# A decode kernel's weight stream: row 31 of wo on another queue, and fifteen marking loads

## The chip, the cores and the metric

The kernel runs on one core of a Trainium2 chip. The metric is the device time of one execution in microseconds (us). The kernel before takes 101.78 us, the median of two runs (101.76 and 101.81). One more execution was recorded by the hardware profiler; its span, from the first to the last instruction, is 100.0 us (100.03).

## What is computed

One token (batch 1, sequence 1, width 1024) goes through a layer with two parallel branches. Cut to what matters:

```python
xn = layernorm(x)
# branch A: attention over the last W = 4096 cached positions, 32 query heads, 4 key/value heads
q = xn @ wq
p = softmax(q . k / sqrt(128));  o = p . v
a = o.reshape(1, 1, 4096) @ wo
# branch B: an MLP, 1024 -> 3584 -> 1024
h = gelu(layernorm(xn) @ w1 + b1)
b = h @ w2 + b2
out = x + a + b
```

All tensors are bf16. With one token every weight is used once, so the kernel reads some 40 MB from memory and does little with each byte.

## The kernel before

**The stream.** SP issues all large loads in one order: the keys (L72), wq in two halves (L81), w1 in two halves (L207), the values (L213), w2 in two halves (L221), wo in two halves (L229). Each large tile is one of four buffers of a ring, so a load waits until an earlier user of its buffer is done; the second half of wo, for instance, takes the buffer that L320 (`o_all`) has read. ScalarE issues three small loads (x, b2, b1) at the start.

**wo and the end.** wo is seen as 128 partitions x 32 rows of 1024, and a row of it (256 KB, 2 KB in each partition) is one step of the final product: `o8[:, c]` against row c. The first half, rows 0 to 15, is one load of 4 MB. The second half, rows 16 to 31, comes in five pieces, cut at 8, 12, 14, 15 and 16, so that the last pieces are small. The list `chunk_src` names the rows in the order in which TensorE uses them: 28 rows of w2, then rows 0 to 31 of wo. All but the last four are summed in `accf` (L341), each row as two products of 512 columns. That sum is copied out (L345 on ScalarE, L346 on VectorE) while the last four rows (`TAIL = 4`, L357) go into fresh sums `acct`, each row as four products; four more products at L353 bring one part of the copied sum back in, before the row next to the last. L361 and L362 make the result, and two halves of the output, 1 KB each, are written by SP (L364) and ScalarE (L365). The program ends (L391) when each queue has seen its landings and the engines have met.

**GpSimd.** It makes small constants at the start and takes part in the two layer norms: `rstd` (L145) and `rstd2` (L168). Between these two stand three selects (L110, L115, L117). VectorE's `yT` (L170) waits for `rstd2`, and behind it on VectorE stand the transposes of the keys (L186) and the copies into `kT` (L202).

**Who sets the order.** Each engine and each queue runs its instructions in order. The tile framework places the instructions of a queue and adds a wait on a semaphore wherever an instruction touches bytes that an earlier one writes; a load's semaphore is raised when its data have landed.

Of the kernel before, what the change touches and what calls it, by code (L numbers as in the profile page):

```python
# [9 lines left out]
BF16 = mybir.dt.bfloat16  # L10
# [6 lines left out]
def kernel(  # L17
# [14 lines left out]
    nc = tc.nc  # L32
    P = 128
    D = A_x.shape[-1]
# [13 lines left out]
    CWO = NQ // P  # L48
# [5 lines left out]
    consts = ctx.enter_context(tc.tile_pool(name="consts", bufs=1))  # L54
# [8 lines left out]
    def ring_tile(name):  # L63
        return ring.tile([P, RING_ELEMS], BF16, tag="ring", name=name, align_bytes=256)
# [13 lines left out]
    for i in range(2):  # L78
        t = ring_tile(f"wq{i}")
        tv = t[:].rearrange("p (r n) -> p r n", r=4)  # L80
# [88 lines left out]
    yT = consts.tile([P, C], BF16)  # L169
    nc.vector.tensor_scalar(out=yT[:], in0=xn_f[:], scalar1=mean2[:], scalar2=rstd2[:], op0=ALU.subtract, op1=ALU.mult)  # L170

    accf = ps_acc.tile([P, 512], FP32, tag="accf")
    nc.vector.memset(accf[:], 0.0)
    accq = ps_acc.tile([P, 2, 512], FP32, tag="accq", name="accq")
# [15 lines left out]
    for g in range(Hkv):  # L190
        T4 = scr[:, g, :].rearrange("p (c a j) -> p c a j", a=4, j=32)
        k = 0
# [11 lines left out]
    for i in range(2):  # L204
        t = ring_tile(f"w1{i}")
        tv = t[:, :4 * Fd].rearrange("p (r n) -> p r n", r=4)
# [8 lines left out]
    chunk_src = []  # L215
    w2_v = B_w2.rearrange("(p c) n -> p c n", p=P)
    for i in range(2):
        nr = CW2 // 2
        t = ring_tile(f"w2{i}")
        tv = t[:, :nr * D].rearrange("p (r n) -> p r n", r=nr)  # L220
        nc.sync.dma_start(out=tv, in_=w2_v[:, nr * i:nr * (i + 1), :])  # L221
        chunk_src += [("h", nr * i + r, tv[:, r, :]) for r in range(nr)]
    wo_v = A_wo.rearrange("(p c) n -> p c n", p=P)
    for i, cuts in enumerate([[0, 16], [0, 8, 12, 14, 15, 16]]):
        nr = CWO // 2
        t = ring_tile(f"wo{i}")
        tv = t[:].rearrange("p (r n) -> p r n", r=nr)
        for a, b in zip(cuts[:-1], cuts[1:]):
            nc.sync.dma_start(out=tv[:, a:b, :], in_=wo_v[:, nr * i + a:nr * i + b, :])  # L229
        chunk_src += [("o", nr * i + r, tv[:, r, :]) for r in range(nr)]  # L230


    for i, w3 in enumerate(wq_tiles):
        for r in range(4):
            c = 4 * i + r
# [16 lines left out]
    for i, w3 in enumerate(w1_tiles):  # L252
        for r in range(4):
            c = 4 * i + r
# [141 lines left out]
```

## Time and profile before

| what | value |
|---|---|
| median of the runs | 101.78 us |
| profiled execution, its span | 100.0 us |
| bytes read from memory | 39.86 MB |
| SP's queue, share of 16 DMA engines over the span | 93.6% |
| busy share: PE, VectorE, ScalarE, GpSimd | 51%, 50%, 34%, 4% |
| last wait of SP for its own output's landing | 0.6 us |

The page gives busy time by engine, the span in 40 slices, and the chain of waits that ended last. The DMA engines are busy in nearly every slice, the compute engines only in some. Times inside the span count from its start. A group row names the line, the engine, the operation, the tiles and the idle time before it with what ended it.

### The profile page before, as it was taken

To read this page: it belongs to the slowest core of one execution; us is meant where nothing else is said; L and a number is where in the kernel's file an instruction comes from. 1 tells how busy PE (TensorE), PEld (TensorE's weight loads), DVE (VectorE), ACT (ScalarE), POOL (GpSimd) and SP (SyncE) were. 2 spreads that over 40 slices of the span, in tenths; PEclk is the share of its full clock that TensorE was granted. 3 is DMA by queue.
4 is the path that set the end of the run, shared out by engine and by line. 5 is a ranking of instruction groups with operands and counts; after the bars stand their busy time and mean duration, and the time that the engine had idled before them with its cause. 6 is when DMAs were issued, how large, how long until landed. Compare 5 with 4: busy or idle time off the path is not lost.

```text
span 100.0 us, 970 instructions
## 1 busy us (share of the span) xinstructions
PE 51.2 (51%) x365; PEld 20.0 (20%) x365; DVE 49.7 (50%) x92; ACT 34.1 (34%) x37; POOL 3.8 (4%) x16
## 2 busy tenths in 40 slices
PE   0065200008500940193892935999469950199980
PEld 0042200002100310031530322334123410033320
DVE  5445499999999999997125115410450000000021
ACT  5000002999999999962001044400000000000010
POOL 6005200000000000000000000000000000000000
PEclk9999999999995579555555555559985998557999
DMA  2999999999999999998999999999999999999920
GB/s 26 394 420 426 491 488 472 419 419 419 432 419 393 401 500 382 413 482 378 390 429 426 429 531 390 413 477 390 459 447 426 419 432 419 406 419 411 401 73 1
DMA packets 2878, 39.92 MB, mean 399 GB/s; under 512 B 309, under 2 KB 311, under 8 KB 698
## 3 DMA queue, kind: packets, MB, share of 16 engines
q1 hardware_dynamic: 2866, 39.85, 93.6%
q8 instruction: 3, 0.05, 0.2%
q10 hardware_dynamic: 8, 0.01, 0.0%
q14 instruction: 1, 0.01, 0.0%
HBM read 39.86 MB, written 0.00 MB: 398 GB/s over the span
## 4 chain that ended last, share of the span: by engine, by line
DVE 38%; DMA 24%; PE 21%; issue 9%; POOL 3%; ACT 2%; SPq 1%; POOLq 1%; ACTq 0%
DMA wo<-in_A_wo_dram 24%; DVE kt_scr L186 17%; DVE kT L202 16%; PE o_all L320 10%; PE sp L276 4%; PE acch L258 3%; ACT e L298 1%; DVE eTb L300 1%; PE qT_ps L262 1%; DVE m_loc L284 1%; PE acct L357 1%; SPq L229 1%; DVE q_sb L241 1%; POOLq L391 1%; POOL spread L110 1%
## 5 line engine op out<-in xcount | busy, mean ns | idle before, releaser
L200 ACT COPY kT<-kt_scr 32x1024 bf16<-32x1024 bf16 x26 | 27.1, 1042 | 14.8 <-DVE kt_scr L186 14.5
L186 DVE STREAM_TRANSPOSE kt_scr<-k_sb 128x4096 bf16<-128x4096 bf16 x4 | 17.4, 4411 | 0.0
L238 PE MATMUL accq<-wq,xnT 128*1 128x512 bf16 x64 | 7.1, 622 | 18.3 <-DMA wq<-in_A_wq_dram 18.3
L202 DVE COPY kT<-kt_scr 32x1024 bf16<-32x1024 bf16 x38 | 15.9, 419 | 0.5
L346 DVE COPY bulk<-accf 33x320 f32<-33x320 f32 x1 | 0.5, 483 | 21.9 <-ACT bulk L345 21.9
L341 PE MATMUL accf<-wo,o 128*1 128x512 bf16 x56 | 8.3, 459 | 6.0 <-DMA wo<-in_A_wo_dram 5.9
L345 ACT COPY bulk<-accf 33x192 f32<-33x192 f32 x1 | 0.3, 312 | 31.9 <-PE accf L341 31.9
L320 PE MATMUL o_all<-v_sb,eTb 128*32 128x512 bf16 x32 | 10.0, 491 | 1.0 <-DVE zcol L311 1.0
L258 PE MATMUL acch<-w,yT 128*1 128x448 bf16 x64 | 6.3, 572 | 6.0 <-DMA w<-in_B_w_dram 6.0
L341 PE MATMUL accf<-w,hT 128*1 128x512 bf16 x56 | 7.9, 451 | 0.0
L238 PEld LDWEIGHTS <-xnT 128*1 128x1 bf16 x64 | 2.1, 116 | 22.5 <-issue 22.4
L320 PEld LDWEIGHTS <-eTb 128*32 128x32 bf16 x32 | 3.8, 120 | 6.9 <-issue 3.9
L341 PEld LDWEIGHTS <-o 128*1 128x1 bf16 x56 | 2.8, 97 | 11.4 <-issue 9.2
L258 PEld LDWEIGHTS <-yT 128*1 128x1 bf16 x64 | 2.0, 115 | 9.8 <-issue 9.8
L276 PE MATMUL sp<-kT,qm 128*32 128x512 bf16 x32 | 3.8, 630 | 0.3 <-DVE qm L267 0.3
L341 PEld LDWEIGHTS <-hT 128*1 128x1 bf16 x56 | 2.7, 96 | 4.7 <-issue 2.5
L323 DVE TENSOR_TENSOR o_m<-o_all,grs 32x512 f32<-32x512 f32 x1 | 0.7, 680 | 5.8 <-PE o_all L320 5.8
L123 PE MATMUL x_ps<-ones_bf,xb 1*128 1x1 bf16 x8 | 0.7, 200 | 5.0 <-DMA xb<-in_A_x_dram 5.0
L298 ACT ACTIVATE e<-sc,nmx 128x1024 bf16<-128x1024 f32 x1 | 1.1, 1148 | 5.7 <-DVE nmx L295 5.7
L315 DVE STREAM_TRANSPOSE hT<-h_sb 128x896 bf16<-128x896 bf16 x1 | 1.7, 1706 | 2.4 <-ACT h_sb L313 2.4
L276 PEld LDWEIGHTS <-qm 128*32 128x32 bf16 x32 | 2.1, 133 | 1.4 <-issue 0.9
L281 ACT COPY sc<-sp 128x512 f32<-128x512 f32 x1 | 0.6, 585 | 4.8 <-PE sp L276 4.8
(88 smaller groups left out, 35.9 us busy)
## 6 DMA issues: line engine op xcount, KB each, us to landing
w<-in_B_w_dram SPq DMA_DIRECT2D x4, 3584.0 KB
wq<-in_A_wq_dram SPq DMA_DIRECT2D x2, 4096.0 KB, 27.0
k_sb<-in_A_k_cache_dram SPq DMA_DIRECT2D x4, 1024.0 KB, 7.1
wo<-in_A_wo_dram SPq DMA_DIRECT2D x1, 4096.0 KB, 29.4
v_sb<-in_A_v_cache_dram SPq DMA_DIRECT2D x1, 2048.0 KB, 19.2
v_sb<-in_A_v_cache_dram SPq DMA_DIRECT2D x2, 1024.0 KB, 23.1
wo<-in_A_wo_dram SPq DMA_DIRECT2D x1, 2048.0 KB
wo<-in_A_wo_dram SPq DMA_DIRECT2D x1, 1024.0 KB
```

Source lines behind the costliest of these rows:

```text
L110: nc.gpsimd.affine_select(out=spread[:], in_=spread[:], compare_op=ALU.not_equal, fill=1.0, base=0, pattern=[[-1, 4], [1, P]], channel_mul ...
L186: nc.vector.transpose(out=scr[:, g, :], in_=k2[:, g, :])
L200: nc.scalar.copy(out=dst, in_=src)
L202: nc.vector.tensor_copy(out=dst, in_=src)
L229: nc.sync.dma_start(out=tv[:, a:b, :], in_=wo_v[:, nr * i + a:nr * i + b, :])
L238: nc.tensor.matmul(accq[32 * t:32 * t + 1, b, :], lhsT=xnT[:, c:c + 1], rhs=w3[:, r, j * 512:(j + 1) * 512], start=(c == 0), stop=(c == C ...
L258: nc.tensor.matmul(acch[32 * t:32 * t + 1, b, :NH], lhsT=yT[:, c:c + 1], rhs=w3[:, r, j * NH:(j + 1) * NH], start=False, stop=(c == C - 1) ...
L276: nc.tensor.matmul(sp[32 * R:32 * R + 32, :], lhsT=qm[:, g, :], rhs=kT[:, g, c0:c0 + 512], start=(g == 0), stop=(g == Hkv - 1), tile_posit ...
L298: nc.scalar.activation(out=e128[:], in_=sc[:], func=ACT.Exp, bias=nmx[:], scale=scale, accum_out=l_loc[:])
L315: nc.vector.transpose(out=hT[:], in_=h_sb[:].rearrange("p (d c) -> p c d", c=CW2))
L320: nc.tensor.matmul(o_all[:].rearrange("h g d -> h (g d)"), lhsT=eTb[:, 32 * c:32 * c + 32], rhs=v4[:, :, c, :], start=(c == 0), stop=(c == ...
L341: nc.tensor.matmul(accf[32 * half:32 * half + 1, :], lhsT=vec[kind](c), rhs=wap[:, half * 512:(half + 1) * 512], start=False, stop=(idx == ...
```

## The change

Row 31 of wo gets a tile of its own, `w_last`, loaded by GpSimd; in the source the load stands behind `yT`, in GpSimd's compiled order between L145 and L110. SP's last cut of wo ends at row 30. In the list of rows, 31 is put ahead of rows 16 to 30, so the last four rows are now 27 to 30. Behind the stream SP issues fifteen loads into a tile `marks` that nothing reads: the k-th takes k partitions of 512 + 32k elements from row 0 of wo. Their shapes differ, so that each can be told in a trace.

```diff
+    w_last = consts.tile([P, D], BF16)
+    nc.gpsimd.dma_start(out=w_last[:], in_=A_wo.rearrange("(p c) n -> p c n", p=P)[:, CWO - 1, :])
     accf = ps_acc.tile([P, 512], FP32, tag="accf")
...
-    for i, cuts in enumerate([[0, 16], [0, 8, 12, 14, 15, 16]]):
+    for i, cuts in enumerate([[0, 16], [0, 8, 12, 14, 15]]):
...
-        chunk_src += [("o", nr * i + r, tv[:, r, :]) for r in range(nr)]
+        rows = [("o", nr * i + r, tv[:, r, :]) for r in range(nr)]
+        if i == 1:
+            rows = [("o", CWO - 1, w_last[:])] + rows[:nr - 1]
+        chunk_src += rows
+
+    marks = consts.tile([16, 1024], BF16)
+    for k in range(1, 16):
+        nc.sync.dma_start(out=marks[0:k, 0:512 + 32 * k], in_=wo_v[0:k, 0, 0:512 + 32 * k])
```

The compiled order of SP's queue from the last piece of wo on, with the landings that each waits for among the marks and the engines:

```
wo, row 30
mark 1
mark 2      waits for mark 1
output      waits for VectorE (L361) and ScalarE (L362)
mark 3      waits for mark 2
mark 4      waits for mark 3
...
mark 15     waits for mark 14
closing waits, mark 15 and the output among them
```

## The prediction

> **What bounds the kernel now.** I read the DMA rows of the page first, then engine and DMA shares by stretch, the last 30 us of the chain of waits, SP's own rows and waits, and GpSimd's rows around the place where it gets a new load. By stretch, the columns are start and end, length, busy time and count of PE, PEld, DVE, ACT and POOL, granted clock, DMA share, GB/s:
>
> ```profile
> 3.00:93.00 90.00, 47.03 (x325) 18.59 (x327) 47.10 (x85) 31.95 (x33) 2.06 (x5) 0.75 1.00 430
> 95.00:96.00 1.00, 0.80 (x10) 0.24 (x8) 0.03 (x1) 0.31 (x1) 0.00 (x0) 1.00 0.45 162
> 96.00:97.00 1.00, 1.00 (x16) 0.35 (x13) 0.46 (x1) 0.00 (x0) 0.00 (x0) 1.00 0.08 29
> ```
>
> For 90 us the 16 DMA engines have a share of 1.00 at 430 GB/s: the kernel is one stream of 39.85 MB without holes. It ends raggedly: at 96 to 97 us a share of 0.08, a little over one engine of 16, still works. The chain, in order of time (start, length, what):
>
> ```profile
> 72.11 23.63 DMA wo<-in_A_wo_dram
> ...
> 96.81 0.55 PE acct L357 x6
> ...
> 97.38 0.48 DVE res L361
> ```
>
> Behind the stream come only the last rows' products, one addition and the output. SP, which issues the stream, has long been done by then; its DMA rows (start, length, line, count), then its waits:
>
> ```profile
> 57.86 15.63 SPq L229 DMA_DIRECT2D wo<-in_A_wo_dram  x6
> 97.93 0.31 SPq L364 DMA_DIRECT2D out_dram<-res  x1
> ```
>
> ```profile
> SPq L364 <- DVE res L361: 24.4, 1, 24.4
> SPq L391 <- DMA out_dram<-res: 0.6, 1, 0.6
> ```
>
> The reader should see two things: SP stands still for 24.4 us before it may issue the output, and the program cannot end before SP has seen the output's landing (L391).
>
> **Row 31 moved to GpSimd.** One issue of 256 KB leaves SP's queue and the same 256 KB come through GpSimd's. In a stretch with share 1.00 there is no hole for it, so the bytes ahead of the end are the same: 256 KB / 430 GB/s = 0.61 us are taken at the front and given back at the tail. Each piece of wo lands up to 0.61 us later, and the last (now row 30) when row 31 did. The packets stay 2 KB. Nothing gained, and the stream's end at 97.0 stands.
>
> The products change order a little. The piece with rows 28 and 29 lands some 0.6 us later than its forerunner (95.74 by the chain, where DMA ends and L357 begins), that is at about 96.35, which is when the old row 30 was there. So row 29 joins row 30 in what comes after the four products of L353 (0.42 us), and one more row, 0.21 us by the spacing of L357's rows, stands in front of the output. I take +0.2 us, with 0 (the laggard engine still decides alone) and +0.4 (two rows) as ends. The output is then issued at 97.93 + 0.2 = 98.13.
>
> GpSimd issues the load between these rows (start, length):
>
> ```profile
> 8.50 0.55 POOL L145 TENSOR_TENSOR rstd<-ve,mhalf 128x1 f32<-128x1 f32 x1 [6.13 <-DVE ve L143]
> 9.03 0.63 POOL L110 TENSOR_SCALAR_AFFINE_SELECT spread<-spread 32x512 bf16<-32x512 bf16 x1
> ...
> 9.87 0.21 POOL L117 TENSOR_SCALAR_AFFINE_SELECT gmask<-gmask 32x4 f32<-32x4 f32 x1
> 11.53 0.55 POOL L168 TENSOR_TENSOR rstd<-ve,mhalf 128x1 f32<-128x1 f32 x1 [1.45 <-DVE ve L166]
> ```
>
> Queued behind it are L110, L115, L117 and L168; DVE's yT and the whole run of transposes (from 12.4 us) wait for L168. GpSimd is idle for 1.45 us before L168, so an issue up to that long is hidden. No row of this trace shows a GpSimd load; the nearest issues are SP's, 0.31 to 0.70 us. I take 0: even a longer one is covered again, since PE sits 5.9 us before L341 waiting for wo (the page's L341 row) and wo's last tile is issued at 71.27 with wo0's landing, at 87.2, still ahead of it. It starts to cost beyond 1.45 + 5.9 = 7.3 us.
>
> **The marks.** By size they are nothing: rows 1 to 15, k rows of 512 + 32k bf16, are 2 x (512 x 120 + 32 x 1240) = 202,240 bytes, 0.47 us at 430 GB/s, behind the last weight. What counts is the compiled order on SP. All fifteen write `marks[0:k, ...]`, so each overlaps the one before, and mark k+1 carries a wait for the semaphore of mark k's landing. The order is: last piece of wo, mark 1, mark 2 (waits for mark 1), the output (waits for res), mark 3 (waits for mark 2), and so on to mark 15, then SP's closing waits, which include mark 15. So thirteen loads stand behind the output, one after another, each a full issue-to-landing time with nothing beside it, and the program ends after the last.
>
> No such load stands alone in the trace. Its price, put together from the trace's records of packets and landings:
> - From start of issue to the first packet: the output on SP started at 97.93, its packet at 98.76: 0.83 us (ACT's twin 97.94 to 98.65: 0.71; the first key load 0.80 to 1.81: 1.01).
> - The packet itself: 1 to 2 KB. A 2 KB packet takes 0.084 us in the stream. Alone, a read takes longer: an 8 KB instruction fetch before the span took 0.549 us where 8 KB in the stream take 0.309, so +0.24. The first packets of the keys took 1.1 to 1.3 us, +0.8 to 1.0. I take 0.08 + 0.24 = 0.32, the fetch being nearest to a lone small read.
> - From packet end to landing: 98.80 to 99.20 for the output, 0.40; 0.34 for the last piece of wo (96.66 to 97.00). 0.37.
> - Wait and next start: 0.05 (SP's next instruction starts 0.02 us after the landing, and an event wait and its gap to the next is 0.06).
>
> Sum 0.83 + 0.32 + 0.37 + 0.05 = 1.57; I take 1.6 us a mark, a little for the slowest of several engines. Ends: 1.2 (ACT's 0.71, no read latency, 0.34) and 2.4 (1.01 + 1.0 + 0.40 + 0.05). These are wide; the chain's thirteen steps multiply them.
>
> The Trainium skill ("DMA: Bandwidth & Descriptors", Anatomy of one DMA) speaks against a chain of small transfers: it puts a fixed 2.0 us on each DMA, measured for loads issued from GpSimd, most of it the receipt of the write. By that figure the marks would cost 13 x 2.0 = 26 us, an estimate from that page; the output's 1.27 us (97.93 to 99.20) is below it here. My sum does not use it.
>
> Start of the chain: SP is free at 98.13 + 0.31 = 98.44. Mark 1 sits behind the stream on its engine and lands by 97.1 at the latest (the stream's last landing is 97.0), mark 2 one cycle later, by 98.7. So mark 3 starts between 98.5 and 98.7, say 98.6. Thirteen cycles: 98.6 + 20.8 = 119.4. The close takes 100.03 - 99.20 = 0.83 as before, plus two more event waits behind mark 15's (0.07 each), 0.96 together: a span of 120.4, 20.3 more than 100.0 (rounded from 100.03). The profiled span lies 1.75 us under the median of the runs, 101.78; that stays. **Forecast 101.8 + 20.3 = 122.1 us.**
>
> **Rivals.**
> 1. A lone small load costs 1.85 us or more, because the cold read of the first key packets (+0.9) is the rule for every idle read and not a start-up effect. For it: each mark finds an idle engine. Against: the second eight engines' first key packets took 0.31 to 0.39 us. At 2.05: 98.7 + 26.7 + 0.96 = 126.3, so 128.1 us; from 1.85 on, 125.4. The skill's 2.0 us (same section) lies in this case. Chance 0.17.
> 2. GpSimd's issue exceeds its cover of 7.3 us: DVE's run, the scores and PE's last products slip. At 10 us it adds 2.7: 124.8 us. Nothing in the trace shows such an issue; SP's longest is 1.2 us (L213). Chance 0.03.
> 3. The other side, not slower: the marks' landings are already counted when SP comes to the waits, because they run through in SP's 24.4 us of idling before the output, and just 0.47 us of bytes is added behind the last weight, off the path: 101.8 to 102.5 us. It decides if thirteen steps cost under 2.0 us, 0.15 us each. Against: thirteen of them stand behind the output in an in-order queue, and SP's shortest DMA issue alone is 0.31 us. Chance 0.01.
> 4. The change does not do what it says, the marks being free of each other: rival 3's time again and inside its chance, for the compiled waits speak against it.
>
> **How the numbers follow.** Forecast, under 1.85 us a mark, 0.79. A cycle of 1.3 gives 98.5 + 16.9 + 0.96 = 116.4, 118.1 us; the range reaches from there to rival 1's 2.05, 128.1 us: 118 to 128. Left out are some 0.07 below 1.3, 0.07 above 2.05 and rival 3. About 2%, 2.0 us, can be told from no change here; faster by that would need the stream itself to shrink, and its ragged tail (95.0 to 97.0) is worth less than 2.0: 0.01. Within 2%: 0.01. Slower: 0.98.
>
> **What would show it.** The stretch 3 to 93 still at share 1.00 and about 430 GB/s; the output issued at 98.1 within 0.4; then thirteen single issues on SP at equal spacing of 1.6 us, all other engines idle; the span 120.4. GpSimd's L168 still near 11.5 to 12. Wrong if the marks' spacing is not 1.3 to 1.85, if the output itself is issued later than 98.6, or if the spacing grows with the number of partitions.

## The result, and the profile after

The changed kernel takes 122.25 us (122.05 and 122.44, two runs), the kernel before 101.78. The ratio is 1.2015, with a 95% interval from 1.1964 to 1.2066: slower by a fifth. The forecast was 122.1. The profiled execution has a span of 120.7 us, where the one before had 100.0.

By stretch (start and end, length, busy time and count of TensorE's products, PE, and weight loads, PEld, of VectorE, ScalarE and GpSimd, granted clock, DMA share, GB/s) the changed kernel shows:

```profile
3.00:93.00 90.00, 44.03 (x315) 17.72 (x317) 46.73 (x85) 31.95 (x33) 2.75 (x6) 0.77 1.01 429
95.00:96.00 1.00, 1.00 (x14) 0.43 (x10) 0.00 (x0) 0.00 (x0) 0.00 (x0) 1.00 0.56 219
96.00:97.00 1.00, 0.98 (x14) 0.40 (x10) 0.05 (x1) 0.31 (x1) 0.00 (x0) 1.00 0.20 63
98.00:121.00 23.00, 0.13 (x4) 0.00 (x0) 0.48 (x1) 0.31 (x1) 0.00 (x0) 0.60 0.04 9
```

The stream is what it was: 90 us at full share and 429 GB/s. The loss is the last line: 23 us with a DMA share of 0.04 and 9 GB/s, in which no engine computes after the result is made. The page's 40 slices, each now 3.0 us long, show the same in one look; the tail is the last eight:

```profile
DMA  2999999999999999899999999999999600000000
GB/s 71 411 431 432 433 525 394 456 413 456 391 456 398 399 418 446 383 429 426 460 452 442 437 427 418 449 434 434 391 429 395 278 13 3 5 8 10 13 17 10
```

SP's rows tell who works there (start, length, line, count), and its waits for whom it waits:

```profile
96.53 0.25 SPq L239 DMA_DIRECT2D marks<-in_A_wo_dram  x1
98.64 0.24 SPq L373 DMA_DIRECT2D out_dram<-res  x1
98.97 19.33 SPq L239 DMA_DIRECT2D marks<-in_A_wo_dram  x13
```

```profile
SPq L239 <- DMA marks<-in_A_wo_dram: 39.1, 13, 23.9
SPq L400 <- DMA marks<-in_A_wo_dram: 1.2, 1, 1.2
```

Mark 2 is issued at 96.53, the output at 98.64, and behind it thirteen marks stretch over 19.33 us up to the end of the last issue; then the closing wait (L400) stands for the landing of the fifteenth. Of the 39.1 us in the first wait, 23.9 belong to mark 2, which waited for mark 1 beside the stream and cost nothing.

The chain of waits must be read with care here. Its last pieces, in order of time, are these:

```profile
56.37 31.89 DMA wo<-in_A_wo_dram
...
88.30 8.27 PE accf L350 x56
...
98.09 0.48 DVE res L370
```

The chain ends at 98.57, with the last instruction that computes. The 22 us behind it are issues and waits of a queue, which are not counted as busy, so the view that should name the cause does not contain it. The span against the end of the chain, and SP's own waits, do.

The growth of the span adds up from SP's rows and the landings, which the trace keeps as steps of the loads' semaphores. The output is issued 0.71 us later (98.64 against 97.93), and 0.33 us pass to the start of mark 3 (98.97). Thirteen links of the chain, each one mark from its issue to its landing and the next issue, take 20.75 us, to the landing of mark 15 at 119.72. The close, from there to the end at 120.73, takes 1.01. Less the 2.10 us that lay between the output's issue and the end before, this is 20.70 us, from 100.03 to 120.73.

### The profile page after: what moved, and what is told of

Read it like the earlier page. It is cut to its first block, busy times and chain, and to the rows that moved or that the text cites. A ratio compares the mean times of both kernels' runs of the same rounds, so it can differ in the third digit from the quotient of the medians.

```text
span 120.7 us, 993 instructions
## 1 busy us (share of the span) xinstructions
PE 49.1 (41%) x365; PEld 19.7 (16%) x365; DVE 49.4 (41%) x92; ACT 34.1 (28%) x37; POOL 4.5 (4%) x17
## 4 chain that ended last, share of the span: by engine, by line
DVE 30%; DMA 26%; PE 14%; issue 6%; POOL 3%; POOLq 1%; ACT 0%
DMA wo<-in_A_wo_dram 26%; DVE kt_scr L188 14%; DVE kT L204 13%; PE accf L350 7%; PE sp L285 3%; PE acch L267 2%; DVE m_loc L293 1%; PE qT_ps L271 1%; PE acct L366 1%; DVE q_sb L250 1%; POOL w_last L173 1%; POOL spread L110 1%; POOLq L400 1%; ACT sc L290 0%; POOL rstd L145 0%
## 5 line engine op out<-in xcount | busy, mean ns | idle before, releaser
L350 PE MATMUL accf<-wo,o 128*1 128x512 bf16 x54 | 8.2, 469 | 4.8 <-DMA wo<-in_A_wo_dram 4.8
L329 PE MATMUL o_all<-v_sb,eTb 128*32 128x512 bf16 x32 | 8.9, 446 | 2.8 <-DMA v_sb<-in_A_v_cache_dram 2.8
L350 PE MATMUL accf<-w,hT 128*1 128x512 bf16 x56 | 8.1, 451 | 2.8 <-DMA w<-in_B_w_dram 2.8
L267 PE MATMUL acch<-w,yT 128*1 128x448 bf16 x64 | 5.5, 509 | 6.5 <-DMA w<-in_B_w_dram 6.5
L350 PEld LDWEIGHTS <-o 128*1 128x1 bf16 x56 | 2.9, 97 | 10.2 <-issue 8.0
L350 PEld LDWEIGHTS <-hT 128*1 128x1 bf16 x56 | 2.8, 96 | 7.7 <-issue 5.5
```

Of the source, the lines that this page charges most:

```text
L267: nc.tensor.matmul(acch[32 * t:32 * t + 1, b, :NH], lhsT=yT[:, c:c + 1], rhs=w3[:, r, j * NH:(j + 1) * NH], start=False, stop=(c == C - 1) ...
L329: nc.tensor.matmul(o_all[:].rearrange("h g d -> h (g d)"), lhsT=eTb[:, 32 * c:32 * c + 32], rhs=v4[:, :, c, :], start=(c == 0), stop=(c == ...
L350: nc.tensor.matmul(accf[32 * half:32 * half + 1, :], lhsT=vec[kind](c), rhs=wap[:, half * 512:(half + 1) * 512], start=False, stop=(idx == ...
```

## The experiments

Each ran beside the kernel before on the same chip; its median was 101.77 to 101.90 there.

### Row 31 alone, and the marks alone

The changed kernel without its marks:

```diff
-    marks = consts.tile([16, 1024], BF16)
-    for k in range(1, 16):
-        nc.sync.dma_start(out=marks[0:k, 0:512 + 32 * k], in_=wo_v[0:k, 0, 0:512 + 32 * k])
```

> Row 31 moved to GpSimd, no marks. Theory (the marks' chain is the whole loss): 101.8 to 102.6 us; the profile of the changed kernel, where the output was issued 0.7 us later than before, points to 102.4, my prediction's own term (+0.2) to 102.0. Rival (the GpSimd load disturbs the stream or VectorE's run and carries some us of the loss): 104 us or more.

Measured: 102.28 us, ratio 1.006 (1.0037 to 1.0082), that is 0.4 to 0.8 us slower. In its profile, taken in one of the two shortest of its eight runs (102.09 us), the output is issued at 98.04.

The other half puts the same marks into the kernel before, with row 31 left last on SP's queue:

> The fifteen marks as in the change, row 31 left last on SP's queue. Theory: the output at 97.9 as before, then 13 marks of 1.6 us and the close, 98.3 + 20.8 + 0.96 = 120.0 of span, 121.7 us. Rival (the two parts need each other, or the move of row 31 carries part): under 120 us.

Measured: 121.13 us, ratio 1.192 (1.1885 to 1.1954). SP's rows from the output on:

```profile
97.90 0.24 SPq L367 DMA_DIRECT2D out_dram<-res  x1
98.23 18.88 SPq L234 DMA_DIRECT2D marks<-in_A_wo_dram  x13
```

The two halves nearly add up: 0.5 us for row 31 and 19.4 for the marks give 19.9 of the 20.5. The 0.6 that is left is not settled: the changed kernel's two runs lie 0.4 us apart, and in its profile the output is issued 0.6 us later than with row 31 alone (98.64 against 98.04) and the thirteen links take 0.5 us more than with the marks alone (20.75 against 20.26). The marks are the loss, and they need no GpSimd load for it.

### The same marks without the chain

In the changed kernel, each mark on partitions of its own:

```diff
-    marks = consts.tile([16, 1024], BF16)
+    marks = consts.tile([P, 1024], BF16)
     for k in range(1, 16):
-        nc.sync.dma_start(out=marks[0:k, 0:512 + 32 * k], in_=wo_v[0:k, 0, 0:512 + 32 * k])
+        p0 = k * (k - 1) // 2
+        nc.sync.dma_start(out=marks[p0:p0 + k, 0:512 + 32 * k], in_=wo_v[0:k, 0, 0:512 + 32 * k])
```

> The changed kernel with each mark on partitions of its own, so that no mark waits for the one before it; same bytes. The compiled order now has all fifteen ahead of SP's half of the output; the seventh waits for row 30's landing (a semaphore used again), eight more follow. Theory (the time is in the waits, not in bytes or issues): some 9 issues of 0.3 us between about 97.4 and 100.1, then the output: about 104 us, 18 us less than the change. Rival (fifteen small loads cost about 1.5 us each however they are ordered): 120 us or more.

Measured: 104.71 us, ratio 1.0286 (1.026 to 1.0312). The same fifteen loads with the same bytes cost 2.9 us in place of 20.5. Nine of them are now issued back to back, and the output behind them:

```profile
96.75 3.35 SPq L240 DMA_DIRECT2D marks<-in_A_wo_dram  x9
100.21 0.24 SPq L374 DMA_DIRECT2D out_dram<-res  x1
```

ScalarE's half of the output went out at 97.98 in this run, SP's half at 100.21. So even these were not free: SP's half stood in the queue behind marks that had waited for row 30's landing, because a semaphore was used again (row 30 landed at 96.73).

Four or five marks, placed so that they do not wait for each other and, but for the last of the five, not for the last pieces of the stream, show what is left. In the kernel before, with row 31 last:

```diff
+    marks = consts.tile([P, 1024], BF16)
+    for p0, k in ((0, 7), (7, 8), (15, 15), (32, 16)):
+        nc.sync.dma_start(out=marks[p0:p0 + k, 0:512 + 32 * k], in_=wo_v[0:k, 0, 0:512 + 32 * k])
```

> The kernel before with four marks of 7, 8, 15 and 16 partitions behind the stream, on partitions that do not overlap, row 31 last as before; they wait only for loads that land long before the stream's end. Theory (marks that nobody waits for and that do not wait for each other are free): within 0.5 us of the kernel before, 101.8 to 102.2. Rival (any mark behind the stream delays the end by its own 1.5 us or more): 103.3 us or more. The marks' packets also tell which DMA engines finish last: a mark of k partitions runs on k engines, so the number of late packets of 7, 8, 15 and 16 tells whether a late engine is the eighth or the sixteenth.

Measured: 102.07 us, ratio 1.0025 (1.001 to 1.004). The output is issued at 97.90, as before:

```profile
71.43 20.85 SPq L234 DMA_DIRECT2D marks<-in_A_wo_dram  x4
97.90 0.24 SPq L368 DMA_DIRECT2D out_dram<-res  x1
```

The quarter of a microsecond that is left fits the close: SP looks at its semaphores in pairs, 0.06 us each, and here four of these looks came after the output's landing (99.25 to 99.50) that had come before it, or not at all. The second set, of 9, 11, 12, 13 and 14 partitions, agrees:

> The kernel before with five free marks of 9, 11, 12, 13 and 14 partitions behind the stream. By the marks of 7, 8, 15 and 16 two of the engines after the eighth end their part of the stream at 96.4 to 96.6, one us behind the rest; which two is open. A mark of k partitions has a late packet (after 96.2) for each late engine among its first k: if they are the last two, none of these marks has one; if, say, the ninth and the fourteenth, the mark of 9 has one and the mark of 14 two. Time: 101.8 to 102.4 us (free marks, five more waits in the close at 0.06 us); rival (a mark delays the end by 1.5 us): over 103.3 us.

Measured: 102.12 us, ratio 1.0021 (1.0006 to 1.0036). What the two say of late engines stands at the end.

### How the price goes with links, partitions and place

Seven marks instead of fifteen, five of them behind the output:

```diff
-    for k in range(1, 16):
+    for k in range(1, 8):
```

> The change with marks 1 to 7 alone, five of them behind the output. Theory (each link behind the output costs its own 1.5 to 1.6 us): mark 7 landed at 106.6 in the changed kernel's trace, so a span of 107.6 and 109.2 us. Rival (a fixed cost that does not go with the number of links, such as a late fetch or the closing of the program): near 122 us; rival (cost goes with the marks' bytes, of which the first seven hold a quarter): about 107 us.

Measured: 108.89 us, ratio 1.0698 (1.0677 to 1.072). SP's rows:

```profile
98.59 0.24 SPq L373 DMA_DIRECT2D out_dram<-res  x1
98.93 6.09 SPq L239 DMA_DIRECT2D marks<-in_A_wo_dram  x5
```

The output and the first mark behind it stand where they stood with fifteen; five marks follow, not thirteen. Eight links less took off 122.25 - 108.89 = 13.4 us, 1.67 each; in the changed kernel's profile the last eight take 1.64 each. The cost goes with the number of links.

Fifteen marks, each of one partition and 544 elements:

```diff
-        nc.sync.dma_start(out=marks[0:k, 0:512 + 32 * k], in_=wo_v[0:k, 0, 0:512 + 32 * k])
+        nc.sync.dma_start(out=marks[0:1, 0:544], in_=wo_v[0:1, 0, 0:544])
```

> The change with every mark the same: one partition, 544 elements. Still a chain of fifteen, thirteen behind the output. Theory (a mark's price is nearly all fixed: issue, way to the first packet, landing): the one-partition mark's own rows (mark 2, on two engines, took 1.26 us from issue to landing) give 1.25 to 1.45 us a link, so 118 to 120.5 us. Rival (the price goes with partitions or bytes, of which a sixth is left): under 112 us.

Measured: 117.53 us, ratio 1.154 (1.1512 to 1.1569), just under the lower end of what the theory expected. SP's rows:

```profile
98.21 0.24 SPq L373 DMA_DIRECT2D out_dram<-res  x1
98.55 15.29 SPq L239 DMA_DIRECT2D marks<-in_A_wo_dram  x13
```

From 98.55 to the last landing at 114.81 thirteen links take 1.25 us each. These thirteen marks move 14,144 bytes in place of 198,848, a fourteenth (the sixth in the expectation was a slip). So 1.25 of 1.60 us stays when partitions and bytes go; the rest goes with the two, which this run cuts together and does not separate.

Both halves of the output issued by ScalarE:

```diff
-    nc.sync.dma_start(out=out_v[0:1, :], in_=res[0:1, :])
+    nc.scalar.dma_start(out=out_v[0:1, :], in_=res[0:1, :])
```

> The change with both halves of the output issued by ScalarE, so that nothing but marks stands on SP behind the stream. Theory (the end is the chain's end, wherever the output stands): mark 3 starts when mark 2 has landed, at 97.8 in place of 99.0, so about 1.2 us less than the change: 121.0 us. Rival (the output held up in SP's queue is what is paid for): 103 to 104 us.

Measured: 120.58 us, ratio 1.1838 (1.1806 to 1.1869), 1.7 us under the change. Mark 3 starts at 97.75 instead of 98.97, right behind mark 2's landing (97.68), which is 1.2 of the 1.7 us; the thirteen links took 0.4 us less in this profile (20.34 against 20.75). The output goes out at 98.25 and 98.52, over 20 us before the program may end. The end is the chain's end, not the output's.

### The chain beside the stream

The same chain issued by GpSimd, fourteen of its marks behind GpSimd's last computation:

```diff
-        nc.sync.dma_start(out=marks[0:k, 0:512 + 32 * k], in_=wo_v[0:k, 0, 0:512 + 32 * k])
+        nc.gpsimd.dma_start(out=marks[0:k, 0:512 + 32 * k], in_=wo_v[0:k, 0, 0:512 + 32 * k])
```

> The same fifteen marks with the same chain of waits, issued by GpSimd, fourteen of them behind its last computation at about 12 us and beside the stream. Theory (a chain costs only what sticks out behind the last work): even at 3 us a link it is over by 55 us, so the time is that of row 31's move alone, 102.0 to 102.8 us. Rival 1 (the links get so slow beside the stream or VectorE that the chain ends behind 100 us): over 6 us a link, more than 104 us. Rival 2 (the marks slow the stream or VectorE down): 103.5 us or more with the chain over long before the end.

Measured: 106.25 us, ratio 1.0427 (1.0391 to 1.0463). This was a miss for the theory as I had priced it. GpSimd's rows (start, length; in brackets how long it waited, and for what):

```profile
83.00 0.50 POOL L239 DMA_DIRECT2D marks<-in_A_wo_dram  x1 [6.48 <-DMA marks<-in_A_wo_dram]
89.60 0.50 POOL L239 DMA_DIRECT2D marks<-in_A_wo_dram  x1 [6.10 <-DMA marks<-in_A_wo_dram]
95.17 0.51 POOL L239 DMA_DIRECT2D marks<-in_A_wo_dram  x1 [5.08 <-DMA marks<-in_A_wo_dram]
98.92 0.50 POOL L239 DMA_DIRECT2D marks<-in_A_wo_dram  x1 [3.23 <-DMA marks<-in_A_wo_dram]
101.13 0.50 POOL L239 DMA_DIRECT2D marks<-in_A_wo_dram  x1 [1.71 <-DMA marks<-in_A_wo_dram]
```

Beside the stream a link takes 5.3 to 8.6 us, mostly 6 to 7, and behind it 2.2. So rival 1 held: the chain got so slow that its last links stuck out, the last landing at 103.1. The output was itself issued late, at 99.75. Seven marks tell whether a chain that ends inside the stream costs anything:

> Marks 1 to 7 alone, chained and issued by GpSimd. With fifteen on GpSimd a link took 5.3 to 11.8 us beside the stream, the last mark landed at 103.1, and the output itself was issued at 99.75. Here the chain is over by about 60 us. Theory (a chain that ends inside the stream costs nothing, and the 106.25 us were its last links sticking out): the time of row 31's move alone, 102.0 to 102.8 us, output issued near 98.1. Rival (marks beside the stream slow it by some 0.1 us each, which is what held the output back): 102.9 us or more, the first half of wo landing later than 88.3.

Measured: 102.31 us, ratio 1.0058 (1.0037 to 1.0078), the time of row 31's move alone. Its seventh mark is issued at 56.00, and the output at 98.24. Forty-odd microseconds of chained waiting, wholly covered, cost nothing. In the run with fifteen the output came late because the stream did: the piece with rows 28 and 29 landed at 97.86 there and at 96.36 with seven, and the output followed 1.89 and 1.88 us behind. What slowed the stream is not settled: the first half of wo landed at 89.05 and at 87.83, and only marks 8 to 15 differ, with one profile of each.

None of these kernels beats the one before. Row 31 alone is a loss of half a microsecond, and the marks can at best be nearly free.

## Why the prediction was right, and where it was not

**The chain of thirteen marks** was the term that mattered, and it held: 13 x 1.6 = 20.8 us forecast, 20.75 measured from mark 3's issue to mark 15's landing. Its parts were less right than their sum. To the first packet it takes 0.9 us (mark 12: 113.01 to 113.94), where 0.83 was taken. The 0.24 us for the latency of a lone read is not to be seen as a longer packet in the small marks (48 and 51 ns in marks 2 and 3), and a link of one partition takes 1.25 us without it. In its place stands a growth that I had named as a sign of being wrong: the spacing rises from about 1.5 us for the third to the seventh mark to 1.76 for the fifteenth. Marks 2 to 15 land 0.28 to 0.42 us behind the end of their last packet, and it is the packets that spread: from the first one's start to the last one's end 0.10 us pass in mark 4 (1.39 us to the next issue), 0.24 in mark 12 (1.61) and 0.46 in mark 15 (1.76). That the mean of 1.60 came out was luck in part: a term too much and a term left out were of about one size.

The chain started at 98.97, where 98.6 was taken, because the output was late; mark 2 had landed at 97.79.

Rival 1, 1.85 us and more a mark, fell: no mark took that. So did the fixed 2.0 us of the Trainium skill ("DMA: Bandwidth & Descriptors", Anatomy of one DMA), by which the marks would have cost 26 us here, an estimate; it is given for loads issued from GpSimd, and the one link of GpSimd's chain that ran behind the stream took 2.2 us from issue to issue (98.92 to 101.13). For SP's loads the measured 1.25 to 1.76 decides.

**Row 31** is where a step failed: "+0.2 us", with 0.4 as its upper end and an output issued at 98.13. Run alone it costs 0.4 to 0.8 us, and in the changed kernel's profile the output went out at 98.64, just beyond the 98.6 that I had set. The step put the landing of the piece with rows 28 and 29 at about 96.35, and that of the last row where row 31 had landed, at 97.00. In the changed kernel's trace they are 96.76 and 97.42: the stream itself ran late, by 0.4 us. With row 31 alone the piece landed at 96.16, and the chain of waits goes on from there:

```profile
71.59 24.57 DMA wo<-in_A_wo_dram
96.16 0.04 issue
96.20 0.38 PE acct L363 x4
```

From this landing to the output's issue 1.88 us pass, with row 31 alone (96.16 to 98.04) as in the changed kernel (96.76 to 98.64), with marks of one partition (96.33 to 98.21) and with seven marks on GpSimd (96.36 to 98.24). So what follows the landing was priced about right, 1.78 us, and the landing was not. Of the eight profiles with row 31 moved, six have it at 96.1 to 96.4, the changed kernel at 96.76 and the fifteen marks on GpSimd at 97.86. The first half of wo shows the same: "up to 0.61 us later" was forecast, against 87.23 before; in the six it came 0.35 to 0.66 us later, in the changed kernel 1.0 (88.25). Why the stream ran later in that profile is not shown.

TensorE was close to setting the output too. In the changed kernel it ran through its 56 products behind the first half (8.27 us, L350) and came to row 28 at 96.78, as that piece landed. With seven marks on SP it came later than the landing (96.39): the 56 products took 8.73 us, and the output went out at 98.59, 2.20 us behind. The granted clock was at half speed until 93.1 us there, until 92.5 in the changed kernel, 91.1 in the kernel before and 90.3 with row 31 alone.

**GpSimd's issue** was costed at nothing, behind a cover of 1.45 us, and the cover held. Its rows in the changed kernel:

```profile
8.90 0.71 POOL L173 DMA_DIRECT2D w_last<-in_A_wo_dram  x1
9.62 0.65 POOL L110 TENSOR_SCALAR_AFFINE_SELECT spread<-spread 32x512 bf16<-32x512 bf16 x1
...
11.05 0.56 POOL L168 TENSOR_TENSOR rstd<-ve,mhalf 128x1 f32<-128x1 f32 x1 [0.40 <-DVE ve L166]
```

The issue takes 0.71 us, and L168 still waits for VectorE, for 0.40. Rival 2 needed 7.3 us.

**The close** was forecast at 0.96 us and took 1.01. **Rival 3**, the chain already run through when the output is issued, fell with the order of SP's queue: thirteen marks stand behind the output. Four free marks, at 102.07 us, show what it would have been worth. **Rival 4**, the marks free of each other, fell with the issues on SP: each stands behind the landing of the mark before it.

## What to carry to other kernels

A load that nothing reads is free only if nothing waits for it, and the program's end waits for every load. Loads into overlapping bytes form a chain in which each pays its whole way from issue to landing, 1.25 to 1.76 us here; give each its own bytes, keep them few enough that no semaphore is used again beside the last pieces, and look at the compiled order for what stands behind what. Where a chain can't be avoided, it belongs beside work that covers it, with the price of a link taken beside that work (6 to 7 us here) and not alone. And a load moved early in a full stream lets what follows land later, the first half of wo by 0.35 to 1.0 us here, so ask who starts on those landings, not only when the last byte comes.

## What the runs showed of the hardware that was not expected

**Two DMA engines end late.** The stream's ragged tail, 1 us long, is chiefly the work of two of sixteen engines. A mark of k partitions shows k packets of its size, and by the Trainium skill ("DMA: Bandwidth & Descriptors", Why a DMA increments its semaphore by 16 and not by 1) they run on the lowest-numbered k engines; no run here shows the numbers themselves. Queued behind the stream, the marks of 7, 8, 9, 11 and 12 partitions have no packet after 96.2, the mark of 13 has one (96.66), the mark of 15 two (96.38 and 96.56); the mark of 14 was issued at 95.89, too late to tell. On that reading the late ones are the thirteenth and either the fourteenth or the fifteenth. The same page of the Trainium skill (Latency and other measured facts) names the engines numbered 7 and 15, the eighth and the sixteenth, as usually slower, with the descriptor rings of loads issued from GpSimd as its best guess at the cause; here the stream is issued from SP, and on that reading these are not the two.

Why they are late was not tried, but the trace of the kernel before has a hint. The last two of a large load's sixteen landings come 0.3 and 0.5 us behind its first in the load that is complete at 32.6 us, 1.1 and 1.6 in the one at 42.2, 1.0 and 1.5 at 60.4, 1.45 and 1.7 at 69.1, and the same at 97.0. The lag grows in two stretches, and in each of them lies one packet of 16 KB on the queue that the profile calls instruction, at 37.14 and 65.11 us, 0.93 us long. Between these stretches and after them there is no such packet until 95.72, and no growth. The changed kernel's trace has the same two steps, with such packets at 38.16 and 65.11. No run tests it.

**A link beside a full stream.** GpSimd's marks took from issue to landing 1.9 to 11.5 us, with a median of 6.3. Marks 2 to 12, beside the stream, had their first packet 3.6 to 4.5 us after the issue began; the two behind the stream had it after 1.2 us and landed after 1.9 and 2.0.

**VectorE's L146** took 0.60 us before, when GpSimd ran its select L110 at the same time, and 0.23 in the changed kernel, where GpSimd issued its load then. The rows, before and after:

```profile
9.09 0.60 DVE L146 TENSOR_SCALAR xn_f<-xc,rstd 128x8 f32<-128x8 f32 x1 [0.40 <-POOL rstd L145]
```

```profile
8.97 0.23 DVE L146 TENSOR_SCALAR xn_f<-xc,rstd 128x8 f32<-128x8 f32 x1 [0.40 <-POOL rstd L145]
```

VectorE's transposes began at 11.85 instead of 12.32. The stream sets the end, so this gains nothing; that the select is the cause was not tried by itself.
